# Infini-attention block on Trainium2: three 128x128 turns moved from TensorE to VectorE and DMA

## The chip, the cores and the metric

The kernel runs on one core of one Trainium2 chip. A core has TensorE (PE in the rows of the profile; its weight load is a row of its own, PEld), VectorE (DVE), ScalarE (ACT), GpSimd (POOL) and the queues that issue transfers, of which SyncE's (SP) carries nearly all here. Each engine takes its instructions in the order in which they were written down for it; semaphores make one wait for another. The metric is the time of one execution on the device in microseconds (us), as the median of several runs; lower is better.

## The reference

One pre-LayerNorm layer on 2048 tokens of width 1024: an Infini-attention block with 32 heads of 32 channels, worked in four segments of 512 tokens with a memory that is carried from one segment to the next, and then an MLP of width 3584. The change touches the attention alone:

```python
for s in range(N):                                    # N = 4 segments
    qs, ks, vs = q[:, :, s], k[:, :, s], v[:, :, s]   # 32 heads, 512 tokens, 32 channels
    logits = einsum("bhqd,bhkd->bhqk", qs, ks) * scale + mask
    a_dot = einsum("bhqk,bhkd->bhqd", softmax(logits), vs)
    pq = phi(qs)                                      # phi(t) = t + 1 if t > 0 else exp(t)
    num = einsum("bhld,bhde->bhle", pq, M)
    den = einsum("bhld,bhd->bhl", pq, z)[..., None] + 1e-6
    o = g * (num / den) + (1.0 - g) * a_dot
    pk = phi(ks)
    M = M + einsum("bhld,bhle->bhde", pk, vs)         # the memory for the next segment
    z = z + einsum("bhld->bhd", pk)
```

## The kernel before

The work runs in two halves of 1024 tokens (two segments each). A half is: attention, the output projection (`wo_first`, `wo_second`), and the first MLP product; the second MLP product follows once for both. Everything that TensorE multiplies is held as two rounded parts, a high part `h` and a low part `l` (the float32 value minus its high part), and every product is three matmuls: high by high, high by low, low by high.

**Units.** Attention goes over 8 groups of 4 heads (`g`), and in each group over the half's two segments (`sl`; the segment is `s = 2 * half + sl`). One such pair is a unit; there are 32, counted here as 16 * half + 2g + sl. `dense(g, sl, ws, u)` projects one unit's keys, queries and values into PSUM (`kps`, `qps`, `vps`, three tiles of 128 channels by 512 tokens, 24 matmuls of 512 columns each). While it does, `heads(prev)` does the softmax attention of the unit before, one head at a time, in the steps written out in `PLAN`: `q` scores (`pqk`), `n` normalising on POOL (`pr`, line 557), `t` turning the weights by TensorE (`ppt`, line 573, copied out by ACT as `pth`), `s` their low part on DVE (`ptl`), `a` weights times values (`po`, line 593), `o` the sum into `ot`. A head's `t` comes one slot after its `q`, its `a` two slots after.

**The three turns.** The projections give channels on the partitions and tokens along the row. Three tensors of a unit are needed the other way about, and TensorE turns each by four 128x128 transposes against the identity:
- `pk`, phi of the keys (segments 0 to 2): into `pkn` during the value projection (line 453), from PSUM to the parts `pkh` by ACT and `pkl` by DVE.
- `vps`, the values (all segments): copied to SBUF as `vt` by ACT (line 461), turned into `vn` (line 469), from there to the two parts of `vs` by ACT and DVE (lines 471, 472).
- `om`, what the memory returns (segments 1 to 3): turned into `pom` (line 516), copied to `omt` by ACT (line 521), added to `ot` on POOL (line 607).

The second and third belong to `late()`, a generator that is advanced during the next unit's projections. It also queues the small matmuls (`smalls`, line 395): `pm` (phi of the queries by the memory) and `pmm` (phi of the keys by the values, which updates the memory `MZ`). These are put one by one between the steps of the heads by `one_small()`.

**Order.** In attention the order on each engine is not written out by hand: the program is handed in as one sequence, and a scheduler puts each engine's instructions in order by priority and by its own estimates of when operands are there. Later stages are pinned to the written order. PSUM tiles of `ps_dense` (three buffers) hold `kps`, `qps`, `vps`, `pkn`, `vn`, `pom`, `pm` and `pmm` in turn. SP issues, in attention, the transfers that stack keys and queries for the score matmuls (`ks`, `qs`: 24 per unit, line 377), the weights of the next group (`wr`, line 326) and the finished `ot` (line 609).

Of the kernel before, what the change touches and what calls it, by code (L numbers as in the profile page):

```python
# [17 lines left out]
P = 128  # L18
# [21 lines left out]
def raw(ap):  # L40
    return ap.bitcast(F32)


def build(tc, x, wq, wk, wv, wo, beta, w1, b1, w2, b2, out):
# [37 lines left out]
    p1_dram = [dram.tile([P, 512], F32, name=f"p1_dram{j}") for j in range(FB // 2)]  # L82
    h_dram = [[dram.tile([S // P, P, FB // 4, P], F32, name=f"h_dram{i}{s}") for s in range(2)] for i in range(2)]

    acts = {}

    def split(pool, w, hi, lo, hi_eng="vector", lo_eng="gpsimd"):
# [256 lines left out]
    def attention(half, first):  # L344
# [4 lines left out]
        def tmp(name):  # L349
            return ab.tile([P, 512], F32, tag="tmp", name=name, bufs=5)  # L350

        def tmpr(name):
            return ab.tile([P, 512], F32R, tag="tmpr", name=name, bufs=6)

# [47 lines left out]
        def dense(g, sl, ws, u):  # L402
            s = 2 * half + sl
            behind = acts.pop("late", iter(()))
            kps = ws.pop("kps", None)
            if kps is None:
                kps = ps_dense("kps")
                for c in project(ws["k"], sl, "kps", kps):
                    if c >= 2:
                        next(behind, None)  # L410
                    yield
            kh, kl = tmpr("kh"), tmpr("kl")
            nc.scalar.copy(kh, kps)
            nc.vector.tensor_tensor(kl, kps, raw(kh), op=ALU.subtract)
            if s < 3:
                kparts = phi_parts(kps)
            qps = ps_dense("qps")
            for c in project(ws["q"], sl, "qps", qps):
                if c == 0:
                    u["ks"] = stack(kh, kl, "ks", (0, 1, 0))  # L420
                if c == 2 and s < 3:
                    zc = ab.tile([P, 64], F32, name="zc", bufs=2)[:, 0:1]
                    pk = phi_sum(kparts, "pk", zc)
                next(behind, None)
                yield
            qh, ql = tmpr("qh"), tmpr("ql")
            nc.scalar.copy(qh, qps)
            nc.vector.tensor_tensor(ql, qps, raw(qh), op=ALU.subtract)
            if s > 0:
                qparts = phi_parts(qps)  # L430

            vps = ps_dense("vps")
            for c in project(ws["v"], sl, "vps", vps):
                if c == 0:
                    u["qs"] = stack(qh, ql, "qs", (0, 0, 1))
                if s > 0:
                    if c == 2:
                        pq = phi_sum(qparts, "pq")
                    if c == 4:
                        while small:  # L440
                            one_small()
                        pqh, pql = tmpr("pqh"), tmpr("pql")
                        mzh = ab.tile([P, 256], F32R, name="mzh", bufs=1)[:, 0:132]
                        mzl = ab.tile([P, 256], F32R, name="mzl", bufs=1)[:, 0:132]
                        nc.scalar.copy(pqh, pq)
                        nc.gpsimd.tensor_copy(mzh, MZ[:, g, :])
                        nc.gpsimd.tensor_tensor(mzl, MZ[:, g, :], raw(mzh), op=ALU.subtract)
                    if c == 5:
                        nc.gpsimd.tensor_tensor(pql, pq, raw(pqh), op=ALU.subtract)
                if c == 1 and s < 3:  # L450
                    pkn = ps_dense("pkn")
                    for i in range(4):
                        nc.tensor.transpose(pkn[:, i * P:(i + 1) * P], pk[:, i * P:(i + 1) * P], ident)
                    pkh, pkl = tmpr("pkh"), tmpr("pkl")
                    nc.scalar.copy(pkh, pkn)
                if c == 2 and s < 3:
                    nc.vector.tensor_tensor(pkl, pkn, raw(pkh), op=ALU.subtract)
                next(behind, None)
                yield
            vt = tmp("vt")  # L460
            nc.scalar.copy(vt, vps)
            vs = ab.tile([P, 16, 64], F32R, name="vs", bufs=2)
            u["vs"] = vs
            omt = u["omt"] = tmp("omt") if s > 0 else None

            def late():
                vn = ps_dense("vn")
                for c in range(4):
                    nc.tensor.transpose(vn[:, c * P:(c + 1) * P], vt[:, c * P:(c + 1) * P], ident)
                vn3 = vn.rearrange("p (a b) -> p a b", b=DH)  # L470
                nc.scalar.copy(vs[:, :, 0:32], vn3)
                nc.vector.tensor_tensor(vs[:, :, 32:64], vn3, raw(vs[:, :, 0:32]), op=ALU.subtract)
                yield
                if s > 0:
                    om = tmp("om")

                    def memory(i2, ps):
                        pm = ps.rearrange("p (a b) -> p a b", a=2)
                        rg = ab.tile([P, 2, 32], F32, name="rg", bufs=2)[:, :, 0:4]
                        nc.vector.scalar_tensor_tensor(  # L480
                            rg, pm[:, :, 128:132], DEN_EPS, bb[:, 4 * g:4 * g + 4].unsqueeze(1).to_broadcast([P, 2, 4]),
                            op0=ALU.add, op1=ALU.mult)
                        nc.vector.reciprocal(rg, rg)
                        nc.vector.tensor_tensor(
                            om[:, i2 * 256:(i2 + 1) * 256].rearrange("p (a h e) -> p a h e", a=2, h=4),
                            pm[:, :, 0:128].rearrange("p a (h e) -> p a h e", h=4),
                            rg.unsqueeze(3).to_broadcast([P, 2, 4, DH]), op=ALU.mult)

                    for i2 in range(2):
                        smalls("pm", [(lambda ps, ii=ii: ps[:, 256 * ii:256 * ii + 132],  # L490
                                       pqh[:, (2 * i2 + ii) * P:(2 * i2 + ii + 1) * P],
                                       pql[:, (2 * i2 + ii) * P:(2 * i2 + ii + 1) * P], mzh, mzl, True, True)
                                      for ii in range(2)], partial(memory, i2))
                left = len(small)
                if s < 3:
                    def update(pmm):
                        nc.vector.tensor_tensor(MZ[:, g, 0:P], pmm[:, 0:P], MZ[:, g, 0:P], op=ALU.add)  # L497
                        own = MZ[:, g, 0:P].rearrange("p (h e) -> p h e", h=4)
                        nc.gpsimd.tensor_tensor(own, own, hsel.unsqueeze(2).to_broadcast([P, 4, DH]), op=ALU.mult)
                        z = ZC[:, g:g + 1]  # L500
                        nc.gpsimd.tensor_scalar(z, z, zc, None, op0=ALU.add)
                        nc.gpsimd.tensor_scalar(MZ[:, g, 128:132], hsel, z, None, op0=ALU.mult)

                    smalls("pmm", [(lambda ps: ps[:, 0:P].rearrange("p (a b) -> p a b", a=4),
                                    pkh[:, c * P:(c + 1) * P], pkl[:, c * P:(c + 1) * P],
                                    vs[:, 4 * c:4 * c + 4, 0:32], vs[:, 4 * c:4 * c + 4, 32:64], c == 0, c == 3)
                                   for c in range(4)], update)
                total = len(small)
                while len(small) > total - left:
                    yield  # L510
                yield
                if s > 0:
                    pom = ps_dense("pom")
                    for i in range(4):
                        one_small()
                        nc.tensor.transpose(pom[:, i * P:(i + 1) * P], om[:, i * P:(i + 1) * P], ident)
                    if s == 3:
                        yield
                        while acts["pth"][0] < 2:
                            yield  # L520
                    op = nc.scalar.copy(omt, pom)
                    if s == 3:
                        tc.add_manual_dep(op.ins, acts["pth"][1].ins.name, NOSYNC, reason="program order")
                while small:
                    yield
            for _ in behind:
                one_small()
            acts["late"] = late()
# [53 lines left out]
        def av(st, n):  # L582
# [3 lines left out]
            po = st["po"]  # L586
            for jk in (0, 1) if n == 0 else (3, 2):
                w = 512 - P * jk
                v = u["vs"][:, 4 * jk + j, :]
                for part in ("pth", "ptl"):  # L590
                    if (jk, part) != (3, "ptl"):
                        one_small()
# [7 lines left out]
        def av_out(st):  # L600
# [3 lines left out]
            nc.vector.tensor_tensor(ot[b, :], po[0:32, :], ot[b, :], op=ALU.add)  # L604
            if j == 3:
                if u["omt"] is not None:
                    nc.gpsimd.tensor_tensor(ot, ot, u["omt"], op=ALU.add)
                if u["g"] < NG - 1:
                    nc.sync.dma_start(o_dram[u["s"]][u["g"]], ot)
                else:  # L610
# [833 lines left out]
```

## Time and profile before

| | before |
|---|---|
| median of 3 runs | 2302.25 us (2301.9 to 2303.4) |
| span of the profiled execution | 2296.2 us |
| instructions | 35279 |
| PE / DVE / ACT / POOL busy | 99% / 67% / 53% / 48% of the span |
| units' stretches | 60 to 490 us and 890 to 1350 us in the span |

The page gives no separate time for the profiled execution beside its span; the median of the runs stands 6.05 us above that span, and lies around it. A row of the groups reads: line, engine, operation, tile written and tiles read, count, busy time and mean duration of one, then how long the engine was idle just before and what ended that. A row of the timeline begins with the start in the span and the duration. Matmuls overlap, so what one costs on PE is the distance from its start to the next one's start, not its duration.

### The profile page before, as it was taken

To read this page: it belongs to the slowest core of one execution; us is meant where nothing else is said; L and a number is where in the kernel's file an instruction comes from. 1 tells how busy PE (TensorE), PEld (TensorE's weight loads), DVE (VectorE), ACT (ScalarE), POOL (GpSimd) and SP (SyncE) were. 2 spreads that over 40 slices of the span, in tenths; PEclk is the share of its full clock that TensorE was granted. 3 is DMA by queue.
4 is the path that set the end of the run, shared out by engine and by line. 5 is a ranking of instruction groups with operands and counts; after the bars stand their busy time and mean duration, and the time that the engine had idled before them with its cause. 6 is when DMAs were issued, how large, how long until landed. Compare 5 with 4: busy or idle time off the path is not lost.

```text
span 2296.2 us, 35279 instructions
## 1 busy us (share of the span) xinstructions
PE 2270.4 (99%) x11769; PEld 1890.8 (82%) x11769; DVE 1540.3 (67%) x3173; ACT 1225.0 (53%) x2549; POOL 1092.4 (48%) x1134
## 2 busy tenths in 40 slices
PE   8999999999999999999999999999999999999999
PEld 6888888878888888888888887888888888888887
DVE  6777777776655565777777777565566766577563
ACT  6777777775453445777777776363344223322221
POOL 5545555555244442555555556253445554155430
PEclk9999999999999999999999999999999999999999
DMA  6333333345465654433333344466667976476762
GB/s 190 92 85 91 93 89 85 87 120 182 139 204 172 188 165 142 113 91 86 85 87 88 87 111 140 156 211 175 176 188 263 345 243 216 159 253 221 249 234 90
DMA packets 322719, 355.36 MB, mean 155 GB/s; under 512 B 26190, under 2 KB 218730, under 8 KB 322538
## 3 DMA queue, kind: packets, MB, share of 16 engines
q1 hardware_dynamic: 259370, 316.40, 45.4%
q10 hardware_dynamic: 63168, 36.71, 5.3%
q8 instruction: 93, 1.52, 0.3%
q14 instruction: 88, 0.72, 0.1%
HBM read 226.59 MB, written 76.09 MB: 132 GB/s over the span
## 4 chain that ended last, share of the span: by engine, by line
PE 91%; ACT 3%; POOL 2%; DVE 2%; issue 1%; DMA 1%; ACTq 0%; SPq 0%; POOLq 0%; DVEq 0%
PE po L1278 22%; PE bps L882 9%; PE cps L882 7%; PE dps L882 6%; PE po L593 6%; PE ppt L573 6%; PE pqk L541 3%; PE vps L116 2%; PE vps L115 2%; PE kps L115 2%; PE kps L116 2%; PE vps L117 2%; PE kps L117 2%; PE pwo L117 2%; PE pwo L116 2%; PE pwo L115 2%
## 5 line engine op out<-in xcount | busy, mean ns | idle before, releaser
L557 POOL TENSOR_SCALAR pr<-pr,nm,gate 128x128 f32<-128x128 f32 (+3 forms) x512 | 322.6, 639 | 345.9 <-DVE nm L554 260.0
L550 ACT ACTIVATE pr<-pr,mx 128x256 f32<-128x256 f32 (+3 forms) x512 | 287.6, 562 | 161.9 <-DVE mx L542 158.2
L580 DVE TENSOR_TENSOR ptl<-ppt,pth 128x512 fp32r<-128x512 f32 (+1 forms) x384 | 227.2, 599 | 86.2 <-ACT pth L575 82.0
L542 DVE CUSTOM_DVE_ANT_0 pr<-pqk,mask 128x256 f32<-128x256 f32 (+3 forms) x512 | 243.3, 484 | 46.5 <-PE pqk L541 43.7
L573 PE MATMUL ppt<-ident,pr 128*128 128x128 f32 x1280 | 223.6, 277 | 2.1 <-POOL pr L557 1.4
L575 ACT CAST pth<-ppt 128x512 fp32r<-128x512 f32 (+1 forms) x384 | 194.2, 517 | 39.0 <-PE ppt L573 33.1
L1288 DVE TENSOR_TENSOR c<-c,po 128x512 f32<-128x512 f32 x160 | 105.4, 683 | 143.1 <-PE po L1278 135.5
L573 PEld LDWEIGHTS ppt<-ident,pr 128*128 128x128 f32 x1280 | 164.6, 140 | 32.5 <-POOL pr L557 2.6
L541 PE MATMUL pqk<-ks,qs 96*128 96x256 f32 (+3 forms) x512 | 161.3, 315 | 0.0
L92 POOL TENSOR_TENSOR wl<-wr,wh 128x1024 fp32r<-128x1024 f32 x52 | 124.5, 2393 | 70.8 <-PE pqk L541 27.6
L593 PE MATMUL po<-pth,vs 128*64 128x512 f32 (+3 forms) x512 | 155.4, 326 | 0.3 <-ACT pth L575 0.2
L593 PE MATMUL po<-ptl,vs 128*64 128x512 f32 (+3 forms) x512 | 153.9, 310 | 1.3 <-DVE ptl L580 1.2
L1278 PE MATMUL po<-w2h,zh 128*128 128x512 f32 x378 | 121.1, 390 | 0.8 <-DVE zh L1218 0.4
L1135 POOL TENSOR_TENSOR w2r<-w2r 128x512 f32<-128x512 f32 x54 | 85.4, 1593 | 72.0 <-DVE c L1288 36.9
L541 PEld LDWEIGHTS pqk<-ks,qs 96*128 96x128 f32 x512 | 96.2, 188 | 21.5
L994 POOL TENSOR_TENSOR s<-r 128x512 f32<-128x512 f32 x28 | 43.6, 1559 | 143.4 <-DVE sa L1010 87.1
L882 PE MATMUL bps<-zh,sb 128*128 128x512 f32 x336 | 111.0, 391 | 0.0
L882 PE MATMUL bps<-zh,sa 128*128 128x512 f32 x336 | 110.8, 390 | 0.0
L115 PE MATMUL vps<-yh,wh 128*128 128x512 f32 x256 | 109.4, 427 | 0.9 <-DVE MZ L497 0.9
L115 PE MATMUL kps<-yh,wh 128*128 128x512 f32 (+1 forms) x264 | 110.1, 417 | 0.0
L115 PE MATMUL qps<-yh,wh 128*128 128x512 f32 x256 | 106.8, 417 | 0.0
L1278 PE MATMUL po<-w2h,hl 128*128 128x512 f32 x322 | 103.2, 390 | 0.5 <-POOL hl L1218 0.3
(241 smaller groups left out, 6657.1 us busy)
## 6 DMA issues: line engine op xcount, KB each, us to landing
hr<-h_dram SPq DMA_DIRECT2D x112, 448.0 KB, 5.4
w2r<-in_B_w SPq DMA_DIRECT2D x122, 256.0 KB, 4.4
r<-in_B_w SPq DMA_DIRECT2D x56, 512.0 KB, 4.5
h_dram<-ht ACTq DMA_DIRECT2D x84, 256.0 KB, 3.7
ks<-kh SPq DMA_DIRECT2D x256, 64.0 KB, 2.0
qs<-qh SPq DMA_DIRECT2D x256, 64.0 KB, 2.0
wr<-in_A_wo SPq DMA_DIRECT2D x32, 512.0 KB, 4.0
wx<-in_B_w SPq DMA_DIRECT2D x56, 256.0 KB, 3.5
```

What stands on the lines that cost most here:

```text
L115: nc.tensor.matmul(ps, ah, bh, start=first, stop=False)
L116: nc.tensor.matmul(ps, ah, bl, start=False, stop=False)
L541: nc.tensor.matmul(pqk[:, :n], u["qs"][j][:, i * P:(i + 1) * P], u["ks"][j][:, 0:n], start=True, stop=True)
L542: nc.vector.tensor_tensor_reduce(out=st["pr"][:, offs[i]:offs[i] + n], in0=pqk[:, :n], in1=mask[:, 512 - n:512], op0=ALU.add, op1=ALU.min, ...
L550: nc.scalar.activation(pi, pi, AF.Exp, bias=mx[:, i:i + 1], scale=-1.0, accum_out=mx[:, 4 + i:5 + i])
L557: nc.gpsimd.tensor_scalar(pi, pi, nm[:, 4 + k:5 + k], gate[:, 1, 4 * g + j:4 * g + j + 1], op0=ALU.mult, op1=ALU.mult)
L573: nc.tensor.transpose(ppt[:, o:o + P], pr[:, offs[i] + jk * P:offs[i] + (jk + 1) * P], ident)
L575: acts["pth"] = n, nc.scalar.copy(pth[:, base:base + w], ppt[:, :w])
L580: nc.vector.tensor_tensor(o, x0, x1, op=ALU.subtract)
L593: nc.tensor.matmul(po[:, P * jk:], v, st[part][:, koff[jk]:koff[jk] + w], start=(jk, part) == (0, "pth"), stop=(jk, part) == (2, "ptl"))
L882: nc.tensor.matmul(ps, x_[:, c, :], y_[:, c, :], start=first and c == 0 and n == 0, stop=last and c == 3 and n == 2, skip_group_check=True)
L1278: nc.tensor.matmul(ps, x_[:, k], y_[k], start=opens and k == 0 and i == 0, stop=closes and k == self.KP - 1 and i == 2, skip_group_check=True)
```

## The change

All three turns leave TensorE. The new function `turned(src, to, mid)` lets VectorE transpose the 128x512 tile in 32x32 blocks (`mid`), sends `mid` to a buffer in HBM (`turn_dram`, six in rotation) with one transfer, and brings it back with four, each of which fills 32 partitions from four runs of 128 elements. All five are issued by SP.

- `pk` is turned during the query projection's step 3; ACT makes `pkh` from the result, now in SBUF, and GpSimd `pkl`.
- `vps` is turned straight out of PSUM at the end of the value projection, without `vt`; ACT makes the high part of `vs`, and GpSimd the low part.
- `om` is turned into `omt` at the end of `late()`; the copy by ACT goes.
- Rows come back in the order head, block of tokens; so the readers (`vk`, `pk4`, the index into `vs` in `av`, `ot4`) permute their access patterns to match.
- The buffers `scr` lie in tiles of the pool `zt`, which the output projection uses later.

```diff
--- before.py
+++ after.py
@@ -82,6 +82,7 @@
     p1_dram = [dram.tile([P, 512], F32, name=f"p1_dram{j}") for j in range(FB // 2)]
     h_dram = [[dram.tile([S // P, P, FB // 4, P], F32, name=f"h_dram{i}{s}") for s in range(2)] for i in range(2)]
 
+    turn_dram = [dram.tile([P, 512], F32, name=f"turn_dram{k}") for k in range(6)]
     acts = {}
 
     def split(pool, w, hi, lo, hi_eng="vector", lo_eng="gpsimd"):
@@ -349,6 +350,18 @@
         def tmp(name):
             return ab.tile([P, 512], F32, tag="tmp", name=name, bufs=5)
 
+        scr = [acts["zt"].tile([P, 4, 512], F32, tag=f"t{x_}3", name=f"sc{x_}") for x_ in "hl"]
+
+        def turned(src, to, mid):
+
+            nc.vector.transpose(mid.rearrange("p (c k d) -> p c k d", c=4, k=4), src.rearrange("p (k c d) -> p c k d", c=4, k=4))
+            d = turn_dram[acts.get("turned", 0) % len(turn_dram)]
+            acts["turned"] = acts.get("turned", 0) + 1
+            nc.sync.dma_start(d, mid)
+            for c in range(4):
+                nc.sync.dma_start(to[32 * c:32 * c + 32].rearrange("j (h x) -> j h x", h=4),
+                                  d[:, c * P:(c + 1) * P].rearrange("(h j) x -> j h x", h=4))
+
         def tmpr(name):
             return ab.tile([P, 512], F32R, tag="tmpr", name=name, bufs=6)
 
@@ -421,6 +434,9 @@
                 if c == 2 and s < 3:
                     zc = ab.tile([P, 64], F32, name="zc", bufs=2)[:, 0:1]
                     pk = phi_sum(kparts, "pk", zc)
+                if c == 3 and s < 3:
+                    kn = scr[1][:, 2 + sl]
+                    turned(pk, kn, scr[1][:, sl])
                 next(behind, None)
                 yield
             qh, ql = tmpr("qh"), tmpr("ql")
@@ -447,29 +463,26 @@
                         nc.gpsimd.tensor_tensor(mzl, MZ[:, g, :], raw(mzh), op=ALU.subtract)
                     if c == 5:
                         nc.gpsimd.tensor_tensor(pql, pq, raw(pqh), op=ALU.subtract)
-                if c == 1 and s < 3:
-                    pkn = ps_dense("pkn")
-                    for i in range(4):
-                        nc.tensor.transpose(pkn[:, i * P:(i + 1) * P], pk[:, i * P:(i + 1) * P], ident)
+                if c == 2 and s < 3:
                     pkh, pkl = tmpr("pkh"), tmpr("pkl")
-                    nc.scalar.copy(pkh, pkn)
-                if c == 2 and s < 3:
-                    nc.vector.tensor_tensor(pkl, pkn, raw(pkh), op=ALU.subtract)
+                    pkn = kn.rearrange("p (h k d) -> p k h d", h=4, k=4)
+                    pk4 = [x_.rearrange("p (k h d) -> p k h d", h=4, k=4) for x_ in (pkh, pkl)]
+                    nc.scalar.copy(pk4[0], pkn)
+                if c == 3 and s < 3:
+                    nc.gpsimd.tensor_tensor(pk4[1], pkn, raw(pk4[0]), op=ALU.subtract)
                 next(behind, None)
                 yield
-            vt = tmp("vt")
-            nc.scalar.copy(vt, vps)
+            vn = scr[0][:, 2 + sl]
+            turned(vps, vn, scr[0][:, sl])
             vs = ab.tile([P, 16, 64], F32R, name="vs", bufs=2)
             u["vs"] = vs
             omt = u["omt"] = tmp("omt") if s > 0 else None
 
             def late():
-                vn = ps_dense("vn")
-                for c in range(4):
-                    nc.tensor.transpose(vn[:, c * P:(c + 1) * P], vt[:, c * P:(c + 1) * P], ident)
                 vn3 = vn.rearrange("p (a b) -> p a b", b=DH)
                 nc.scalar.copy(vs[:, :, 0:32], vn3)
-                nc.vector.tensor_tensor(vs[:, :, 32:64], vn3, raw(vs[:, :, 0:32]), op=ALU.subtract)
+                nc.gpsimd.tensor_tensor(vs[:, :, 32:64], vn3, raw(vs[:, :, 0:32]), op=ALU.subtract)
+                vk = vs.rearrange("p (h k) e -> p k h e", h=4)
                 yield
                 if s > 0:
                     om = tmp("om")
@@ -503,24 +516,14 @@
 
                     smalls("pmm", [(lambda ps: ps[:, 0:P].rearrange("p (a b) -> p a b", a=4),
                                     pkh[:, c * P:(c + 1) * P], pkl[:, c * P:(c + 1) * P],
-                                    vs[:, 4 * c:4 * c + 4, 0:32], vs[:, 4 * c:4 * c + 4, 32:64], c == 0, c == 3)
+                                    vk[:, c, :, 0:32], vk[:, c, :, 32:64], c == 0, c == 3)
                                    for c in range(4)], update)
                 total = len(small)
                 while len(small) > total - left:
                     yield
                 yield
                 if s > 0:
-                    pom = ps_dense("pom")
-                    for i in range(4):
-                        one_small()
-                        nc.tensor.transpose(pom[:, i * P:(i + 1) * P], om[:, i * P:(i + 1) * P], ident)
-                    if s == 3:
-                        yield
-                        while acts["pth"][0] < 2:
-                            yield
-                    op = nc.scalar.copy(omt, pom)
-                    if s == 3:
-                        tc.add_manual_dep(op.ins, acts["pth"][1].ins.name, NOSYNC, reason="program order")
+                    turned(om, omt, tmp("omx"))
                 while small:
                     yield
             for _ in behind:
@@ -586,7 +589,7 @@
             po = st["po"]
             for jk in (0, 1) if n == 0 else (3, 2):
                 w = 512 - P * jk
-                v = u["vs"][:, 4 * jk + j, :]
+                v = u["vs"][:, 4 * j + jk, :]
                 for part in ("pth", "ptl"):
                     if (jk, part) != (3, "ptl"):
                         one_small()
@@ -604,7 +607,8 @@
             nc.vector.tensor_tensor(ot[b, :], po[0:32, :], ot[b, :], op=ALU.add)
             if j == 3:
                 if u["omt"] is not None:
-                    nc.gpsimd.tensor_tensor(ot, ot, u["omt"], op=ALU.add)
+                    ot4 = ot.rearrange("p (k c j) -> p k c j", k=4, c=4)
+                    nc.gpsimd.tensor_tensor(ot4, ot4, u["omt"].rearrange("p (c k j) -> p k c j", k=4, c=4), op=ALU.add)
                 if u["g"] < NG - 1:
                     nc.sync.dma_start(o_dram[u["s"]][u["g"]], ot)
                 else:
```

## The prediction

> **What bounds the kernel now.** I read the page first, then the busy time by stretch for the two attention stretches, then who waited for whom, then the timeline.
>
> ```profile
> span 2296.2 us, 35279 instructions
> PE 2270.4 (99%) x11769; PEld 1890.8 (82%) x11769; DVE 1540.3 (67%) x3173; ACT 1225.0 (53%) x2549; POOL 1092.4 (48%) x1134
> ...
> PE 91%; ACT 3%; POOL 2%; DVE 2%; issue 1%; DMA 1%; ACTq 0%; SPq 0%; POOLq 0%; DVEq 0%
> ```
>
> The chain that ended last is TensorE for 91%. The stretches say the same of attention (us, then busy time of each engine), and the waits of PE there come to 2.0 us in the first and none in the second:
>
> ```profile
> 60.00:490.00 430.00, 428.87 (x2610) 362.45 (x2610) 320.11 (x947) 312.26 (x793) 221.17 (x313) 1.00 0.35 89
> 890.00:1350.00 460.00, 457.99 (x2770) 386.97 (x2769) 342.25 (x1009) 336.36 (x837) 253.58 (x342) 1.00 0.37 96
> ...
> PE vps L115 <- DVE MZ L497: 0.9, 1, 0.9
> PE pt L149 <- DVE yl L153: 0.9, 1, 0.9
> PE ppt L573 <- POOL pr L557: 0.2, 1, 0.2
> ```
>
> The reader is to see that TensorE has no slack at all in these 890 us: whatever it no longer issues shortens them, and whatever it newly waits for lengthens them by as much. The others have slack on average: DVE 74%, ACT 73%, POOL 53%.
>
> **Removed from TensorE.** The groups give counts and durations:
>
> ```profile
> L516 PE MATMUL pom<-ident,om 128*128 128x128 f32 x96 | 19.3, 288 | 0.8 <-DVE om L484 0.8
> L469 PE MATMUL vn<-ident,vt 128*128 128x128 f32 x128 | 19.3, 273 | 0.6 <-ACT vt L461 0.6
> L453 PE MATMUL pkn<-ident,pk 128*128 128x128 f32 x96 | 14.4, 272 | 0.0
> ```
>
> That is 96 + 128 + 96 = 320 transposes. Their durations overlap, so I count starts:
>
> ```profile
> 1004.62 0.40 PE L116 MATMUL kps<-yl,wh 128*128 128x512 f32 x1
> 1004.86 0.39 PE L117 MATMUL kps<-yh,wl 128*128 128x512 f32 x1
> 1005.09 0.60 PE L469 MATMUL vn<-ident,vt 128*128 128x128 f32 x4
> 1005.44 0.43 PE L541 MATMUL pqk<-ks,qs 96*128 96x384 f32 x1
> ...
> 1015.86 0.40 PE L117 MATMUL qps<-yh,wl 128*128 128x512 f32 x1
> 1016.09 0.72 PE L516 MATMUL pom<-ident,om 128*128 128x128 f32 x4
> 1016.65 0.60 PE L573 MATMUL ppt<-ident,pr 128*128 128x128 f32 x4
> ...
> 1024.75 0.39 PE L117 MATMUL vps<-yh,wl 128*128 128x512 f32 x1
> 1024.98 0.60 PE L453 MATMUL pkn<-ident,pk 128*128 128x128 f32 x4
> 1025.41 0.38 PE L573 MATMUL ppt<-ident,pr 128*128 128x128 f32 x2
> ```
>
> Four transposes of `vn` take 1005.44 - 1005.09 = 0.35 us, of `pkn` 0.43, of `pom` 0.56; `pom` is cheaper, some 0.3, where it is threaded between small matmuls. With the same difference taken over every group of the trace: `vn` 32 groups, 12.6 us (0.39 each, since what follows starts later too); `pkn` 24 groups, 10.3; `pom` 24 groups, 7.5. Sum **30.4 us**, 0.095 a transpose. [...]
>
> **Added beside TensorE.** Durations of the moved subtractions, on the engine they leave and on the one they join:
>
> ```profile
> L449 POOL TENSOR_TENSOR pql<-pq,pqh 128x512 fp32r<-128x512 f32 x24 | 31.0, 1290 | 27.4 <-ACT pqh L445 26.1 <-DMA qs<-ql 1.3
> L472 DVE TENSOR_TENSOR vs<-vn,vs 128x512 fp32r<-128x512 f32 x32 | 22.0, 686 | 0.7 <-ACT vs L471 0.4 <-DMA qs<-qh 0.3
> L580 DVE TENSOR_TENSOR ptl<-ppt,pth 128x256 fp32r<-128x256 f32 x128 | 53.4, 417 | 3.5 <-ACT pth L575 2.2
> L471 ACT CAST vs<-vn 128x512 fp32r<-128x512 f32 x32 | 18.8, 587 | 26.4 <-PE vn L469 26.4
> ```
>
> POOL gains 24 + 32 = 56 subtractions of 1.29 us, 72 us: 61% of the 890. ACT loses 56 copies of about 0.59, 33 us. DVE loses 56 of about 0.69, 38 us, and gains 80 block transposes, which no row shows. Bounds: 0.42 us (DVE's row of half the width) to 1.29 us (POOL's for the shape); I take 0.69, that of DVE's own 128x512 rows, 55 us, so DVE stands at 76%. [...]
>
> The transfers: 80 turns of five, 400 on SP.
>
> ```profile
> ks<-kh SPq DMA_DIRECT2D x256, 64.0 KB, 2.0
> o_dram<-ot SPq DMA_DIRECT2D x28, 256.0 KB, 2.3
> ...
> L377 SPq DMA_DIRECT2D ks<-kh x256: 507/581/1293, 25.8 to 1364.9; - x128
> ...
> 1032.56 0.48 PE L115 MATMUL kps<-yh,wh 128*128 128x512 f32 x1
> ```
>
> Queue time is 0.58 us each (24 + 12.5 a unit, 21 us of 30), landing 2.0 us for the loads and 2.3 for the store. A turn takes 0.69 + 0.5 + 2.3 + 4 x 0.58 + 2.0 = 7.8 us, or, with the keys' transfers ahead of the loads, some 10. In the order of the changed program ACT takes the returned values next to the next unit's `kh`, one key projection later: 1032.6 to 1042.1 us in the trace, and 1.5 for what ACT does first, so 11 us. It is hidden with 1 to 3 us to spare. Behind SP's waiting loads stand the next `ks`, `qs` and weights; behind ACT's copy the exps and `pth`. The cover is thin, and without it each late us is lost in full (third rival).
>
> **Where TensorE will wait.** In the order of the changed program, in the second half (line numbers of the changed file; L484 is the new subtraction):
>
> ```
> PE    L118 kps | L544 pqk 128 | pm, po ... | L116-118 qps | L544 pqk 384 | L576 ppt x4
>       L408 Matmult pmm<-vs,pkh 128x128 [waits DVE_49,Activation_49]
>       L596 po x2
>       L408 Matmult pmm<-vs,pkh 128x128 [waits Pool_49]
> ACT   L426 kh | L553 exp 256 | L553 exp 128 | L483 TensorCopy vs<-sch | ...
> POOL  L93 wl 1024 | L560 pr 128 | L560 pr 256 | L484 TensorTensor vs<-sch,vs | ...
> ```
>
> The low part of `vs` has moved to POOL, stands there behind a weight subtraction and two `pr`, and TensorE asks for it 0.2 us after the high part. The same steps in the trace of before, from the last key matmul:
>
> ```profile
> 1041.88 0.39 PE L117 MATMUL kps<-yh,wl 128*128 128x512 f32 x1
> 1042.31 0.59 ACT L413 CAST kh<-kps 128x512 fp32r<-128x512 f32 x1 [1.14 <-PE kps L117]
> 1043.20 0.19 ACT L550 ACTIVATION_READ_ACCUMULATOR pr<-pr,mx 128x1 f32 x1
> 1043.34 2.39 POOL L92 TENSOR_TENSOR wl<-wr,wh 128x1024 fp32r<-128x1024 f32 x1 [1.82 <-DVE wh L89]
> 1043.75 0.19 ACT L550 ACTIVATION_READ_ACCUMULATOR pr<-pr,mx 128x1 f32 x1
> 1044.45 0.31 PE L395 MATMUL pmm<-vs,pkh 128*128 128x128 f32 x1
> 1045.72 0.98 POOL L557 TENSOR_SCALAR pr<-pr,nm,gate 128x128 f32<-128x128 f32 x2
> ...
> 230.57 0.39 PE L117 MATMUL kps<-yh,wl 128*128 128x512 f32 x1
> 231.60 2.39 POOL L92 TENSOR_TENSOR wl<-wr,wh 128x1024 fp32r<-128x1024 f32 x1 [1.36 <-PE pqk L541]
> 233.97 1.43 POOL L557 TENSOR_SCALAR pr<-pr,nm,gate 128x128 f32<-128x128 f32 x2
> ```
>
> With 1041.88 as zero: ACT is through the two exps at 2.06 (1043.75 + 0.19), the high part is there 0.59 later, at 2.7; POOL is free at 4.8 (1045.72 + 0.98), the low part is there 1.29 later, at 6.1. TensorE gets to the first `pmm` at 2.57 + 0.3 (all four `ppt` now stand before it) and to the low part at 3.1. It waits **3.0 us**, and behind that matmul all of attention stands still. On POOL itself the next `pr` queue behind the subtraction; `ppt` reads those a slot later, so they add nothing. This holds for segment 2 in groups 3 to 6. In segment 0 of the same groups the order is alike (zero at 230.57, POOL free at 4.8), only that `qps` is placed behind `pmm`: TensorE is there at 2.5, ACT, with one activation of 0.5 us more, at 3.2: it waits 0.7; after one `pmm` and two `qps`, 0.5 us, it waits from 3.7 to 6.1 for the low part. 3.1 together. Eight units by 3.0: 24 us. Segment 1 there has one exp ahead on ACT (read out at 1.5) and nothing on POOL: high part at 2.1, low at 3.45, asked for at 2.95: four by 0.5, 2 us. In seven units of segment 3 the first reader stands some 5 to 9 us further on: nothing. The other thirteen (groups 0 to 2, 7) by the same working come to 0.5 to 3.3 each, 19 us. Sum **45 us**.
>
> The rest I cost at nothing: `pkl` on POOL is read nearly a unit later; `omt` is read at the end of the next unit's heads; ACT's load falls.
>
> **Sum.** 2296.2 - 30.4 + 45 = 2310.8 us of span; with the 6.05 us that the median lies above it, **2317 us**, 0.6% slower. About 4.6 us, 0.2%, is what a measurement of this kernel can tell from none.
>
> **Rivals.** *POOL is in time (faster).* The wait decides, not the work: if the mean wait of the 32 units stays under 30.4 / 32 = 0.95 us, the change gains. It would, if POOL's weight subtraction came before the keys end, or the late matmuls reached TensorE later than counted. With no waits left: 2272 us. For: TensorE hardly waits for POOL today, and the scheduler moves things to suit. Against: the order is fixed in the program, and POOL's 1.29 us is the mean of 24 rows. Chance 0.19. *A draw*, within 4.6 us: 0.08. *SP cannot keep up (much slower).* ACT's copy of the values waits for the loads, and the exps and `pth` queue behind it. At 1.5 us in each of 32 units 48 us more: 2365 us. For: SP is taken to 21 of 30 us and stands still for each store. Against: the spare time above. Chance 0.14. [...] Chance 0.03. That the transposes remain is excluded: the changed program has 320 fewer matmuls. My forecast keeps 0.56; its own range is 2306 to 2332.
>
> **Numbers.** Range 2282 to 2350: it leaves out the lower half of the first rival (0.10), the page's price (0.03) and the upper half of the queue's (0.07). Faster 0.19 + 0.03 = 0.22; same 0.08; slower 0.56 + 0.14 = 0.70.
>
> **What would show it.** In the profile after: no `pkn`, `vn`, `pom`; PE waits of some 45 us in attention, nearly all `pmm` behind POOL's low part of `vs`, 3 us each in groups 3 to 6; DVE block transposes near 0.7 us; SP's loads landing in 2 us, before ACT asks. I am wrong if those waits are under 20 us, or if PE waits for ACT's high part, which would put the fault on the transfers.

## Result: 4.2% slower, and the profile after

The changed kernel takes 2399.82 us (median; 2392.81 to 2402.14), against 2302.07 us for the kernel before on the same chip: a ratio of 1.042, 95% interval 1.040 to 1.044. The forecast was 2317 us, with a range to 2350. The direction was right, the size was not: 97.8 us were lost where 14.6 were forecast. The profiled execution took 2398.02 us, its span 2396.2.

The page of the changed kernel, the lines that answer to those of before, and the row of the granted clock by slices (all nines before):

```profile
span 2396.2 us, 35311 instructions
PE 2299.4 (96%) x11449; PEld 1896.9 (79%) x11449; DVE 1554.9 (65%) x3197; ACT 1192.9 (50%) x2493; POOL 1172.6 (49%) x1190
PEclk9989999998999999999999999999999999999999
...
PE 62%; DVE 3%; POOL 2%; ACT 2%; DMA 1%; issue 1%; SPq 1%; ACTq 0%; POOLq 0%; DVEq 0%
```

TensorE has 320 matmuls fewer and yet 29 us more of busy time (2299.4 against 2270.4), beside some 71 us more in which it is idle. The chain that ended last is TensorE for 62% only. The stretches of attention show the reason for the odd busy time (the third column from the right is the granted clock, 1.00 in both before):

```profile
60.00:500.00 440.00, 407.06 (x2245) 336.94 (x2246) 293.88 (x850) 267.13 (x687) 242.04 (x311) 0.94 0.46 121
890.00:1380.00 490.00, 466.87 (x2558) 385.72 (x2557) 337.34 (x936) 302.46 (x735) 263.15 (x334) 0.97 0.48 131
```

So there are two losses: waits of TensorE, and a lower clock while it works. Who waited for whom (us in total, times, the longest):

```profile
PE pmm L408 <- POOL vs L484: 30.9, 17, 2.9
PE ppt L576 <- DVE ptl L583: 8.3, 8, 1.7
PE pmm L408 <- ACT vs L483: 6.8, 11, 1.5
PE pmm L408 <- ACT r L377: 6.7, 5, 1.7
PE pm L408 <- POOL pql L465: 5.8, 3, 3.3
PE ppt L576 <- POOL pr L560: 5.4, 9, 1.4
PE po L596 <- POOL vs L484: 2.7, 2, 2.1
```

The waits for the two parts of `vs` come to 30.9 + 6.8 + 2.7 = 40.4 us, close to the 45 that the forecast has. The others were in no step of it. One unit of segment 0, group 3, in the timeline of the changed kernel:

```profile
262.40 2.38 POOL L93 TENSOR_TENSOR wl<-wr,wh 128x1024 fp32r<-128x1024 f32 x1 [1.04 <-PE po L596]
263.60 0.61 ACT L483 CAST vs<-sch 128x512 fp32r<-128x512 f32 x1
264.26 0.33 PE L408 MATMUL pmm<-vs,pkh 128*128 128x128 f32 x1 [0.33 <-ACT vs L483]
264.75 1.50 POOL L560 TENSOR_SCALAR pr<-pr,nm,gate 128x128 f32<-128x128 f32 x2
266.22 1.26 POOL L484 TENSOR_TENSOR vs<-sch,vs 128x512 fp32r<-128x512 f32 x1
267.54 0.33 PE L408 MATMUL pmm<-vs,pkh 128*128 128x128 f32 x1 [2.43 <-POOL vs L484]
```

That is the forecast's own picture: the low part behind a weight subtraction and two `pr`, a wait of 0.33 for the high part and of 2.43 for the low. What follows it was not in the picture. The same unit in stretches of 3.4 us (busy time of each engine, then the clock):

```profile
265.10:268.50 3.40, 0.97 (x10) 0.97 (x9) 2.52 (x6) 2.07 (x6) 3.40 (x5) 1.00 0.42 96
268.50:271.90 3.40, 3.40 (x12) 2.82 (x12) 0.29 (x1) 0.00 (x0) 2.79 (x6) 0.50 0.67 195
271.90:275.30 3.40, 3.40 (x20) 2.69 (x19) 1.85 (x6) 1.46 (x4) 0.50 (x2) 1.00 0.74 210
```

TensorE was busy for 0.97 of 3.40 us; in the next 3.4 us it is busy throughout, at half the clock, and gets through 12 matmuls where the stretch behind that has 20. The wait cost 2.43 us, and the clock, if half of the 3.4 us at 0.50 is lost, another 1.7.

**The account of attention.** For each run I took from its trace, for both halves, the time from the first to the last score matmul (`pqk`), the time in that in which no matmul ran, and the time at a granted clock of 0.50, half of which I count as lost: an estimate, from matmuls of 512 columns in e9, which start 0.43 us apart at 0.50 and 0.23 at 1.00. Before: 985.3 us long, 10.2 idle, none at 0.50. The rows below are differences to that, in us; "removed" is the forecast's count of the turns that the kernel no longer has on TensorE, and "left" is what the three do not explain.

| kernel | time (us) | attention | removed | idle | half clock / 2 | left |
|---|---|---|---|---|---|---|
| changed kernel | 2399.8 | +97.4 | -30.4 | +70.0 | +54.6 | +3.2 |
| e1: low part of `vs` on VectorE | 2346.2 | +44.1 | -30.4 | +43.4 | +25.6 | +5.5 |
| e2: low part of `pk` too | 2342.0 | +37.5 | -30.4 | +42.7 | +18.8 | +6.4 |
| e4: as changed, asked for later | 2380.6 | +77.0 | -30.4 | +59.0 | +41.0 | +7.4 |
| e8: values alone | 2346.6 | +47.8 | -12.6 | +32.6 | +27.3 | +0.5 |
| e7: `pk` and `om` alone | 2303.0 | -1.5 | -17.8 | +12.0 | +3.4 | +0.9 |
| e13: `pk` alone | 2303.0 | +1.8 | -10.3 | +7.8 | +3.4 | +0.9 |
| e14: `om` alone | 2295.9 | -3.7 | -7.5 | +4.4 | +1.7 | -2.3 |
| e15: e2, values make no trip | 2308.3 | +5.2 | -30.4 | +25.2 | +10.3 | +0.1 |
| e16: e2, no trips | 2288.3 | -12.7 | -30.4 | +18.6 | 0 | -0.9 |
| e17: changed kernel, no trips | 2279.8 | -22.0 | -30.4 | +7.4 | +1.7 | -0.7 |

The account closes to within 8 us in every row, to 3.2 for the changed kernel. Two things are rough in it. In the 109 us at half clock of the changed kernel TensorE is idle for some 10, which stand in both columns, so the clock's 54.6 may be 5 too high. And the trace of e7 is that of its fastest execution, 2298.5 us, where its median is 2303.0.

### The profile page after: what moved, and what is told of

It reads as the page before. It is cut to its first block, busy times and chain, and to the rows that moved or that the text cites. A ratio compares the mean times of both kernels' runs of the same rounds, so it can differ in the third digit from the quotient of the medians.

```text
span 2396.2 us, 35311 instructions
## 1 busy us (share of the span) xinstructions
PE 2299.4 (96%) x11449; PEld 1896.9 (79%) x11449; DVE 1554.9 (65%) x3197; ACT 1192.9 (50%) x2493; POOL 1172.6 (49%) x1190
## 4 chain that ended last, share of the span: by engine, by line
PE 62%; DVE 3%; POOL 2%; ACT 2%; DMA 1%; issue 1%; SPq 1%; ACTq 0%; POOLq 0%; DVEq 0%
PE po L1282 22%; PE bps L886 9%; PE cps L886 6%; PE dps L886 6%; PE po L596 2%; PE ppt L576 2%; PE pwo L117 1%; PE pwo L118 1%; PE pwo L116 1%; PE pqk L544 1%; PE vps L116 1%; PE vps L117 1%; PE vps L118 1%; PE qps L116 1%; PE kps L117 1%
## 5 line engine op out<-in xcount | busy, mean ns | idle before, releaser
L560 POOL TENSOR_SCALAR pr<-pr,nm,gate 128x128 f32<-128x128 f32 (+3 forms) x512 | 328.5, 650 | 303.6 <-DVE nm L557 243.8
L578 ACT CAST pth<-ppt 128x512 fp32r<-128x512 f32 (+1 forms) x384 | 189.1, 514 | 166.6 <-PE ppt L576 160.9
L576 PE MATMUL ppt<-ident,pr 128*128 128x128 f32 x1280 | 231.1, 283 | 16.8 <-DVE ptl L583 8.3
L116 PE MATMUL qps<-yh,wh 128*128 128x512 f32 x256 | 116.5, 455 | 0.0
L118 PE MATMUL qps<-yh,wl 128*128 128x512 f32 x256 | 109.2, 427 | 1.6 <-POOL wl L93 1.6
```

Source lines behind the costliest of these rows:

```text
L116: nc.tensor.matmul(ps, ah, bh, start=first, stop=False)
L118: acts["mm"] = nc.tensor.matmul(ps, al, bh, start=False, stop=last)
L560: nc.gpsimd.tensor_scalar(pi, pi, nm[:, 4 + k:5 + k], gate[:, 1, 4 * g + j:4 * g + j + 1], op0=ALU.mult, op1=ALU.mult)
L576: nc.tensor.transpose(ppt[:, o:o + P], pr[:, offs[i] + jk * P:offs[i] + (jk + 1) * P], ident)
L578: acts["pth"] = n, nc.scalar.copy(pth[:, base:base + w], ppt[:, :w])
```

## The experiments

**Theory A**: GpSimd's low part of `vs` makes TensorE wait, and each long wait brings half clock behind it. **Theory B**: the round trip through HBM comes too late and holds TensorE by itself. **Theory C**: the clock falls because TensorE was idle, and not for anything else in attention.

### e1, e2: the low parts back on VectorE

```diff
-                nc.gpsimd.tensor_tensor(vs[:, :, 32:64], vn3, ...      # e1
+                nc.vector.tensor_tensor(vs[:, :, 32:64], vn3, ...
-                    nc.gpsimd.tensor_tensor(pk4[1], pkn, ...           # e2: this too
+                    nc.vector.tensor_tensor(pk4[1], pkn, ...
```

> The changed kernel, with the low part of vs back on VectorE (0.69 us there against 1.27 on GpSimd, and no weight subtraction ahead of it). Theory A (GpSimd's low part makes TensorE wait, and each wait of 2 us or more is followed by 3.4 to 6.8 us at half the granted clock): the 33.6 us of waits for GpSimd's vs go, the 71 us of half clock that begin within 1 us of such a wait go with them (35.7 us of time); the mean clock rises from 0.977 to about 0.99 and the time falls by some 64 us to 2336. Theory B (the round trip through HBM comes too late and is what holds TensorE): TensorE then waits as long for ScalarE's high part or for others, the clock stays at 0.98 and the time above 2380.

> As the run before, and the low part of pk on VectorE too, so that GpSimd has no more to do than in the kernel before. Theory A: pkl is read nearly a unit later, so within 10 us of the run before (2326 to 2346). A rival (it is GpSimd's whole load of 72 us, that delays pr, pql and the weights' low parts): the other waits for GpSimd, some 14 us, and the half clock behind them go too, 2315 or less.

Measured: 2346.2 us (ratio 1.020, 1.018 to 1.021) and 2342.0 (1.018, 1.017 to 1.020). The waits of e1:

```profile
PE ppt L576 <- DVE ptl L583: 10.1, 10, 1.7
PE pmm L408 <- ACT vs L483: 6.7, 11, 1.5
PE pm L408 <- POOL pql L465: 5.8, 3, 3.3
PE pmm L408 <- ACT r L377: 5.5, 5, 1.4
PE pmm L408 <- DVE vs L484: 4.7, 4, 1.2
```

The 33.6 us for GpSimd's `vs` are gone, 4.7 for VectorE's have come, the rest stands. Of the 97.8 us lost, 53.6 return, 10 less than theory A had: idle time falls by 26.6 and half clock by 58 (29 in time). `pkl` makes 4 us, little more than the runs scatter, so GpSimd's whole load is not it. Over 40 us remain that theory A does not explain.

### e4: asked for later

```diff
                 vk = vs.rearrange("p (h k) e -> p k h e", h=4)
                 yield
+                yield
+                yield
```

> The changed kernel with GpSimd's low part of vs left where it is, but late() gives way twice more (two steps of the projection, some 2.6 us) before it queues the small matmuls. Theory A: TensorE asks for the low part about as much later as it waits now (2.4 to 2.9 us), so most of the 37 us of waits for vs and the half clock behind them go: 2335 to 2350. Theory B: the waits of TensorE for other engines remain as they are and the time stays above 2380.

Measured: 2380.6 us (1.035, 1.033 to 1.036). The waits of `pmm` for GpSimd fall to 17.5 us (13, up to 3.0), but new ones come, 7.9 us of `pm` behind `om`. The miss is to be read with care: two steps later in the program did not mean 2.6 us later on TensorE, since the scheduler placed everything anew. The same edit on top of e2:

> The run with both low parts on VectorE (2342), and late() gives way twice more, some 2.6 us, before it queues the small matmuls. If what is left is the values' data coming 0.3 to 1.7 us late, the 19 us of waits of pmm for vs and for the buffer go, with the half clock: 2310 to 2322. If the rest is of another kind (other engines' chains that TensorE's turns used to cover), 2330 or more.

Measured: 2346.4 us (1.020, 1.019 to 1.021), no gain over e2.

### e7, e8, e13, e14: one turn at a time on the kernel before

```diff
 # e14 (om alone); e13 and e7 take over the pk lines of the change with pkl on VectorE,
 # e8 the lines for vn, vk and av, with the low part of vs on VectorE
-                    pom = ps_dense("pom")
-                    ...
-                    op = nc.scalar.copy(omt, pom)
+                    turned(om, omt, tmp("omx"))
```

> The kernel before, with pk and om turned by VectorE and DMA (low part of pk on VectorE), and the values turned by TensorE as before, both parts of vs as before. Theory A: no wait for vs, the 17.8 us of TensorE's turns of pk and om are saved, few new waits: 2284 to 2295, clock 1.00. Theory B: the round trips alone make TensorE wait by some 20 us and more, and the clock falls: 2310 or above.

> The kernel before, with the values alone turned by VectorE and DMA (both parts of vs made as before, the low one on VectorE); pk and om stay on TensorE. Turning pk and om alone cost 2 us (2303 against 2301), turning all three with both low parts on VectorE 41 us (2342). Theory A2 (the values' turn alone is late: its loads land behind the weights of the next group, and small matmuls that TensorE meets at once hang on them): all of that belongs to the values, 2330 to 2345, with 15 to 20 us of waits of pmm for vs or for the PSUM bank. Rival (it is the sum of the three turns' transfers on one queue): the values alone take a third of it, 2305 to 2315.

> The kernel before with pk alone turned by VectorE and DMA, its low part on VectorE. TensorE's 10.3 us for pkn go. pk is needed nearly a unit later, so if the round trip is hidden: 2292 to 2297. If taking work from TensorE only uncovers waits for the other engines (as with pk and om together, 17.8 us saved and nothing gained): 2299 to 2304.

> The kernel before with om alone turned by VectorE and DMA; TensorE's 7.5 us for pom go and ScalarE's copy. Hidden: 2294 to 2298. Uncovered waits for other engines: 2300 to 2306.

Measured: `pk` and `om` 2303.0 us (1.0005, 0.9995 to 1.0014), values alone 2346.6 (1.0194, 1.0177 to 1.0211), `pk` alone 2303.0 (1.0007, 0.9998 to 1.0016), `om` alone 2295.9 (0.9983, 0.9974 to 0.9992). The values alone lose as much as all three in e2. In e8, ScalarE's and VectorE's rows (line, tile, count, busy time and mean, then idle time before and what ended it) name what came late, and TensorE's longest wait (us in total, times, the longest) what it brought:

```profile
L480 ACT CAST vs<-sch 128x512 fp32r<-128x512 f32 x32 | 19.9, 621 | 18.1 <-DMA sch<-turn_dram 18.1
L481 DVE TENSOR_TENSOR vs<-sch,vs 128x512 fp32r<-128x512 f32 x32 | 31.9, 996 | 19.9 <-ACT vs L480 19.8
PE pmm L407 <- ACT r L376: 16.4, 7, 3.5
```

ScalarE itself stands still for the loads, 18.1 us, and `r`, which it makes just behind the cast, comes late with it. Turning `pk` away from TensorE gains nothing although 10.3 us of work go, and `om` alone is 4.7 us faster than the kernel before, a small gain whose interval just leaves out 1: the only version here that leaves nothing out and beats both kernels. `pk` and `om` together do not keep that gain.

### e11: is it the PSUM buffer?

`pmm` waits for `r`, the last reader of `kps`, and the buffers of `ps_dense` rotate without `vn` now.

```diff
             def late():
+                nc.tensor.transpose(ps_dense("vn")[:, 0:P], ident, ident)
                 vn3 = vn.rearrange("p (a b) -> p a b", b=DH)
```

> The run with both low parts on VectorE (2342), plus one 128x128 transpose of the identity into a tile of ps_dense at the start of late(), where vn stood, read by nobody: it costs TensorE some 3 us and shifts the rotation of the three PSUM buffers back by one. If the waits of pmm for ScalarE's r (the last reader of kps) are a wait for the buffer (6.8 us in five units, and 16.4 in seven with the values alone), they go and with them some half clock: 2325 to 2338. If r only happens to stand behind the high part of vs on ScalarE, they stay: 2341 to 2350.

Measured: 2344.1 us (1.019, 1.017 to 1.020), the waits for `r` 7.4 us instead of 6.8. So it is not the buffer, as far as this shift of it shows. What else `r` waits for, the next runs narrow down.

### e15, e16, e17: without the round trips

```diff
-            turned(vps, vn, scr[0][:, sl])
+            nc.vector.transpose(vn.rearrange("p (c k d) -> p c k d", c=4, k=4), vps.rearrange("p (k c d) -> p c k d", c=4, k=4))
 # e15: values only, on e2; e16: pk and om in the same way, on e2; e17: all three, on the changed kernel
```

> The run with both low parts on VectorE (2342), in which the values make no trip through HBM: VectorE's 32x32 blocks are written where the loads would have put them and read from there, so the values are only turned within blocks; store and four loads per unit are left out, all engine work is in place. If the values' round trip is what is late: the waits of pmm behind ScalarE's high part and r go, and most of the remaining idle time and half clock, 2285 to 2305. If the missing work of TensorE only uncovers the other engines' chains: 2330 or more.

> As the run before with all three round trips left out (values, pk and om turned within blocks only), all engine work in place. Round trips as the cause: TensorE's 30.4 us of turns are gained and nearly nothing is lost, 2272 to 2290, clock 1.00. Uncovered chains: 2320 or more.

> The changed kernel itself (both low parts on GpSimd) with all three round trips left out in the same way. The wait for GpSimd's low part does not hang on the data's arrival but on the weight subtraction and two pr ahead of it, so 25 to 35 us of waits of pmm for it and 40 to 70 us of half clock stay: 2320 to 2345. If the round trip was behind those waits too, it falls to that of the run before, 2272 to 2290.

Measured: 2308.3 us (1.003, 1.001 to 1.004), 2288.3 (0.994, 0.993 to 0.996) and 2279.8 (0.990, 0.989 to 0.992). The values' trip is worth 34 us in e2, the other two 20. One part of the expectation missed. The waits for the high part go, but those for `r` stay, in e15 and then in e16:

```profile
PE pmm L408 <- ACT r L377: 7.0, 7, 1.1
PE pmm L408 <- ACT r L377: 7.6, 7, 1.1
```

So a late cast ahead of `r` makes the longer ones (up to 1.7 in e2, 3.5 in e8), but a wait of 1.1 is there without any trip; why stays open. And theory A does not hold by itself, against what I expected of e17: with GpSimd's low part in place but no trips, the time is the best of all. A unit of e17:

```profile
278.04 0.72 DVE L476 STREAM_TRANSPOSE sch<-vps 128x512 f32<-128x512 f32 x1
278.79 0.63 ACT L483 CAST vs<-sch 128x512 fp32r<-128x512 f32 x1 [0.15 <-DVE sch L476]
279.50 1.30 POOL L484 TENSOR_TENSOR vs<-sch,vs 128x512 fp32r<-128x512 f32 x1
283.74 0.22 PE L408 MATMUL pmm<-vs,pkh 128*128 128x128 f32 x1
287.88 2.39 POOL L93 TENSOR_TENSOR wl<-wr,wh 128x1024 fp32r<-128x1024 f32 x1 [1.10 <-PE pqk L544]
```

The same 1.3 us on GpSimd are through at 280.8, 2.9 us before TensorE asks, and ahead of the weight subtraction instead of behind it. Over all 32 units the low part is finished 15.3 us after the start of the last value matmul in the changed kernel (median), 4.0 in e17, 5.5 in the kernel before. So GpSimd's queue was the last link, and the trip put the subtraction at that place in it: the scheduler orders by when it expects operands. In the unit of the changed kernel shown above it was this order that was late, and not the data: the last of its four loads landed at 260.23, and ScalarE began the cast at 263.60, though it had stood idle for 1.13 us in between. The same holds for all seven units of groups 3 to 6 in which that wait is 2.4 us or more: the cast begins 0.5 to 4.0 us after the last landing that the trace tells. In e8 the data themselves are late. How the rest divides into arrival and order, these runs do not part.

### e9, e10, e18: idle time and clock alone

Attention is left as before; in the second MLP product, where TensorE is otherwise never idle, it waits for tiny copies of ScalarE.

```diff
+            if n >= acts.get("stall", 6) and self.jobs[n - 1][1] not in "16":
+                acts["stall"] = n + 2                                # e10: n + 5
+                nc.scalar.copy(junk, acts["ps"][:, 0:8])             # behind the product before
+                for _ in range(2):                                   # e10: 10; e18: 1
+                    nc.scalar.copy(ah[:, 0, 0:8], raw(ah[:, 0, 0:8]))
+            acts["ps"] = ps
             for k in range(self.KP):
```

> The kernel before, attention untouched; in the second MLP product, where TensorE is otherwise never idle, TensorE is made to wait some 30 to 40 times for two tiny copies of ScalarE, 0.7 to 1.0 us each, all else equal. Both theories of the clock expect the same here: the waits cost their own length, some 30 us, the granted clock stays at 1.00, and the time is about 2302 + 30 = 2332.

> As the run before with ten copies instead of two, 2.2 to 2.6 us of wait, and fewer of them (every fifth product or so, 15 to 20 times), so that the idle time of TensorE is about the same, 40 us. Theory C (idle time of more than about half of a stretch of 3.4 us halves TensorE's clock for the next 3.4 to 6.8 us): most of these waits are followed by half clock, 50 to 110 us of it in all, which costs 25 to 55 us on top: 2365 to 2395, mean clock 0.98 or less. Rival (the clock falls in attention for another reason, the mix of matmuls or the load of the other engines): clock 1.00 and about 2342.

> The run with short stalls (2431 us, some 50 waits of 1.9 us, 72 us of half clock), with one tiny copy instead of two, so each wait is 0.2 us shorter, about 1.7 us. Theory C with its bound between 1.84 and 1.90 us of idle time in a stretch of 3.41 us: no half clock at all, mean clock 1.00, and the time falls by 10 us of waits and 36 us of half clock to about 2385. Rival (the clock falls by the sum of idle time over a longer stretch, or by chance): half clock as before in proportion, some 60 us of it, and about 2415.

Measured: 2430.9 us (1.056, 1.054 to 1.059), 2408.2 (1.046, 1.044 to 1.048) and 2395.0 (1.041, 1.038 to 1.043). I had sized the waits wrongly: two copies make 1.90 us in most places and 1.3 in others, not 0.7 to 1.0; ten make 3.1 to 6.5. So e9 did not serve as the run without half clock, and served better: first a stretch of e9 with a wait of 1.90 and the one behind it, then the same of e18 with 1.67 (read as above).

```profile
2118.30:2121.70 3.40, 1.50 (x7) 0.95 (x6) 1.40 (x3) 1.44 (x5) 0.00 (x0) 1.00 0.82 231
2121.70:2125.10 3.40, 3.40 (x10) 2.62 (x9) 0.98 (x1) 0.38 (x1) 0.00 (x0) 0.50 0.70 208
```

```profile
1803.50:1806.90 3.40, 1.73 (x8) 1.24 (x7) 3.10 (x4) 1.62 (x4) 2.92 (x2) 1.00 1.00 381
1806.90:1810.30 3.40, 3.40 (x16) 2.82 (x15) 1.82 (x1) 0.00 (x0) 0.87 (x1) 1.00 0.20 67
```

In the changed kernel's trace the clock changes at whole multiples of 3.41 us from its first record, each time, and is at 0.50 for one, two or three of them. If this stage is cut at such steps, then over the three runs each stretch at full clock with 1.90 us or more of idle time in it is followed by half clock (40 of 40), and none with 1.84 us or less (0 of 442). e18's 14 stretches with 1.67 us idle have none behind them; its 17 us of half clock follow four waits that came out at 2.0 to 3.3 us, which is why it came out at 2395 and not 2385. Its 50 waits are 6.2 us shorter in sum than e9's (76.1 against 82.3), and it is 36 us faster. Theory C stands in a stage that has nothing of attention: in these three runs idle time in a stretch of 3.41 us parts the stretches that have half clock behind them from those that have not.

In attention idle time does not settle it alone. Of the changed kernel's 18 falls from full to half clock, 13 follow a stretch with 1.93 us or more of idle time, but five follow one with 1.30 to 1.79, while one with 1.77 has none behind it. What parts the cases better in that trace is the number of columns that the matmuls of a stretch put through (512 for a tile of 512 columns, and of a matmul that crosses a step the part inside). Counted from the first record of the clock on, and without the end of the program, half clock follows all 15 stretches at full clock with fewer than 2600 columns, three of the six between 2743 and 2882, and none of the 643 with more than 3100. This is a count over one trace, and no run was made to test it.

## Why the prediction was wrong, point by point

- **What bounds the kernel.** Right, but the two stretches are confused in one place: the 2.0 us of waits belong to the second, and the view of the first lists none.
- **Removed, 30.4 us.** Right, if slightly high: the difference of starts, summed over the 32 groups of `vn` in the trace of before, is 11.5 us and not 12.6, so 29.3 in all. e17, where nearly nothing is lost, gains 22.0 us in attention with 7.4 idle and 1.7 of clock: -30.4 + 9.1 = -21.3. The price of a transpose behind the chance of 0.03 is shown by no run; by the starts the 320 transposes took these 29.3 us.
- **Block transposes, 0.69 us on VectorE.** Right, 0.71, in the group of the changed kernel; so is GpSimd's 1.29:

```profile
L357 DVE STREAM_TRANSPOSE sch<-vps 128x512 f32<-128x512 f32 x32 | 22.6, 706 | 2.4 <-PE vps L118 1.6
L484 POOL TENSOR_TENSOR vs<-sch,vs 128x512 fp32r<-128x512 f32 x32 | 41.1, 1284 | 27.2 <-ACT vs L483 26.1 <-DMA ks<-kl 1.0
```

- **Round trip, 7.8 to 10 us, loads landing in 2.0.** The values' loads land in 3.7 (median), the other two's in 2.1 and 2.0:

```profile
sch<-turn_dram SPq DMA_DIRECT2D x128, 64.0 KB, 3.7
scl<-turn_dram SPq DMA_DIRECT2D x96, 64.0 KB, 2.1
```

  In groups 3 to 6 the cast of the high part starts 9 to 11 us after the block transpose (one unit 14), in the others 10 to 25. "Hidden with 1 to 3 us to spare" held in segments 0 and 2 of groups 3 to 6 (0.5 to 4.0 us between landing and cast), and failed in segments 1 and 3: there the cast starts within 0.4 us of the landing, and in five units ScalarE stands waiting for it (4.4 us). With the values alone (e8) ScalarE waits 18.1 us, so the rival that the queue cannot keep up had more to it than its 0.14.
- **Where TensorE will wait, 45 us.** The step held in size: 40.4 us, at the places named, 2.9 us in segment 2 of groups 4 to 6 (3.0 forecast; in group 3, where it was forecast too, 0.6 behind GpSimd) and 2.4 to 2.5 us for the low part in segment 0 (2.4 forecast). Only its cause was read too narrowly: I took the place in GpSimd's queue as given, and by e17 it was a consequence of the trip.
- **"The rest I cost at nothing."** Failed. 70.0 - 40.4 = 29.6 us of other idle time in attention: `ppt` behind `ptl` and `pr`, `pm` behind `pql`, `pmm` behind `r`. e7 and e13 show that turning `pk` and `om` away is not free: of the 17.8 us saved, 15.4 come back as idle time and clock. By e15 and e16 it is their trips that make it, 20 us; through which queue or engine stays open, and 1.1 us of `r`'s waits need no trip at all.
- **The sum had no term for the clock.** This is the step that failed most: 54.6 of the 83 us between forecast and result. The step was "whatever it newly waits for lengthens them by as much": each late us was to be lost once, and no more. A wait of 2.4 us cost 4 to 6 by the estimate of the account, with 3.41 or 6.83 us of half clock behind it. The 2.89 us of wait that end at 1324.31, which a step of 3.41 us cuts into 1.77 and 1.12, have no half clock behind them. Nothing in the trace of before showed this price: its clock is 1.00 in both stretches of attention, and its longest wait behind the start 1.1 us.

The rest: 14.6 forecast + 54.6 + 29.6 - 4.6 (45 against 40.4) + 3.2 left = 97.4. Of the conditions set ahead, "waits of some 45 us, nearly all `pmm` behind GpSimd" came true with a time far outside the range: it tested the wait, and nothing tested its price. The other sign, TensorE waiting for ScalarE's high part, showed as well (6.8 us in 11 waits). It points at the transfers, which e15 to e17 bear out, though in segment 0 of groups 3 to 6 the data had landed before.

## What to carry to other kernels

Where one engine has no slack, price a wait on it by what follows as well: on TensorE here a wait of 1.67 us among equal, wide matmuls had no half clock behind it (14 stretches of e18) and cost about itself, one of 2.4 us in attention cost mostly 4 to 6, an estimate with half of the time at 0.50 counted as lost. When a producer is moved off the bound engine, ask first when its result arrives and what that does to the order on all the others; a trip through HBM moved the values' low part from 5.5 to 15.3 us after the projection, and without the three trips the same engine work gains 21 us where it lost 98. Do one part of a bundle at a time: of three turns, one gains a little, one does nothing, and one loses 45 us even with its low part on VectorE.

## What the runs showed of the hardware that I had not expected

- In e9, e10 and e18, where all matmuls of the stage are 512 columns wide, TensorE's granted clock was 0.50 in the 3.41 us behind each of 40 stretches of 3.41 us with 1.90 us or more of idle time, and 1.00 behind each of 442 with 1.84 us or less. In the changed kernel it also fell after 1.30 to 1.79 us (five of 18 falls), and it fell after each of 15 stretches with fewer than 2600 columns put through.
- Beyond idle time and clock e9 lost some 11 us and e18 some 9, over 50 waits each, 0.2 us a wait; the first matmul behind one of e9's waits took 0.50 us where others took 0.39. In e10, with 20 longer waits, nothing of the kind is left over.
- A 128x512 block transpose of float32 took VectorE 0.71 us from PSUM (`vps`) and from SBUF (0.70 for `pk`, 0.71 for `om`) in the changed kernel, about as much as the 0.69 of a subtraction of that shape in the kernel before.
- In the changed kernel the same kind of load (64 KB in runs of 128 elements) landed in 2.0 to 2.1 us for `pk` and `om` and in 3.7 for the values. Of the values' loads whose landing the trace tells, the 59 that shared their time with a transfer of the next group's weights (512 KB each) took 4.9 us (median), the 53 others 2.0. But the 29 loads of `pk` and `om` that did so took no longer than their like, 2.2 and 2.0 us, so the weights alone are not shown to be the cause.
